# Two transformer layers on one core: transposes held back until the fourth row should be normalised, the next block's statistics started before, and a wait of Pool for the fourth normalisation

## The chip, the cores and the metric

One core of a Trainium2 chip runs the whole program. The metric is the device time of one execution in microseconds. The kernel before took 3607.83 us in the median of three runs (3604.56 to 3613.43). TensorE is called PE here, VectorE DVE, ScalarE ACT, GpSimd POOL, and SyncE, which issues nearly all DMAs, SP.

## The reference: two layers of attention and squared-ReLU MLP

The input is 2048 rows of 640 numbers in float32. Each of the two layers computes

```
n = layernorm(x);  q, k, v = n @ wqkv          (32 heads of 20)
x = x + concat_h(softmax(q k^T / sqrt(20)) v) @ wo
n = layernorm(x)
x = x + (relu(n @ w1 + b1) ** 2) @ w2 + b2     (1536 hidden)
```

The same weights serve both layers.

## The kernel before

Every float32 operand of a product is kept as a high and a low part, and a product is made of three: high by high, high by low, low by high. The part that the change touches is the first stage of a layer, in which rows are normalised, transposed and multiplied by wqkv.

**Blocks.** The 2048 rows are four blocks of 512, and a block is four tiles of 128 rows by 640. For a block, `front` (line 381) loads the four row tiles (SP, tile `x`, out of a pool of 11), computes the `stats` of each (line 239: two BATCH_NORM_STATS2 and one aggregate on DVE, then L247 and L248, variance plus eps to the power of -1/2, on POOL), and normalises each in place (L252, on DVE, tile `mv` holds mean and factor). Then 20 transposes on PE (L398) turn the block, five column groups k of four each, into PSUM banks: a group of two k, again two, then one. Each k is split from its bank into the high and low part of `xnT` by one of two ways: `split_to` (ACT casts, L256, and DVE subtracts, L257), or `split_on_pool` (ACT copies to `r`, L263, POOL casts, L271, and POOL subtracts, L274). For some k of blocks 2 and 3 it is POOL. Four banks in a ring (`ps_q`) serve the transposes and the scores.

**Products.** `qkv` (line 679) issues for each of the units (block, column tile of wqkv) a chain of 30 half matmuls (L327, 64 rows of the array each; two chains run in turns). `end_qk` (line 335) takes the finished sums of q or k out of the bank: ACT copies, POOL subtracts into the low part `ev` (L274) and, for k of the odd blocks, forms the difference of two blocks' keys in `kf` (L350) and splits it into `kd` (L271, L274). The tiles are stored to `d_qk` and `d_kd` by SP and loaded again as `k`, `q`, `kd` for the scores (L479). A score matmul fills a bank, and DVE takes the row maximum from it (L491).

**What sets the order.** The program is written out by a planner inside `qkv`. It keeps a model clock for PE, DVE and ACT (`now`); before each half matmul `insert` (line 804) may place one score operation or one group of transposes if the model says that the bank is free. The row work of the blocks is a generator, `rest`: `step_rest` takes one piece of it after every fourth step of the chains (loads, one `stats`, one normalisation), unless `state["turn"]` is set. It is set as soon as the fourth normalisation has been issued, and then the next free place takes the first group of transposes. `fronts` (line 410) loads the next block's rows at the eighth piece of a block. So in the program a block's evictions always stand ahead of the next block's statistics. In layer 1 (`begin_first`, line 1374) block 0 is done apart, and there alone the first POOL subtraction of the weights waits for the fourth normalisation (`lo_later`). In layer 2 (`second`, line 1357) only block 3 goes this way; blocks 0 to 2 arrive transposed from the stage before.

An engine works its own list in order; a wait holds all that is behind it on that engine.

Of the kernel before, what the change touches and what calls it, by code (L numbers as in the profile page):

```python
# [22 lines left out]
KD = D // P  # L23
# [16 lines left out]
def tile_layers(  # L40
# [11 lines left out]
    nc = tc.nc  # L52
# [45 lines left out]
    ps_q = Ring(0, 1, 2, 3)  # L98
# [16 lines left out]
    x_in = a_x[0]  # L115
    x_out = out[0]

    class Split:
# [132 lines left out]
    def normalise(eng, x, mv):  # L251
        return eng.tensor_scalar(x, x, mv[:, 0:1], mv[:, 1:2], op0=ALU.subtract, op1=ALU.mult)  # L252
# [17 lines left out]
    def pool_hi(dst, src):  # L270
        nc.gpsimd.tensor_copy(dst, src)  # L271

    def pool_lo(dst, a, b):
        nc.gpsimd.tensor_sub(dst, a, b)  # L274

    THREE = ((0, 0), (0, 1), (1, 0))

    def row_tile(src, r):
        t = xtile("x")
        dma(nc.sync, t, src[r * P : (r + 1) * P, :])  # L280
        return t
# [96 lines left out]
            v = vs.pop(tt)  # L378
            return lambda: dma(nc.sync, d_v[tt * P : (tt + 1) * P], v)

    def front(tb, x_src, bank, each=1, on_pool=()):

        rows = [row_tile(x_src, tb * 4 + i) for i in range(4)]
        yield 0, False
        mvs = []
        for x in rows:
            mvs.append(stats(x))
            yield 1.1, False
        for n, (x, mv) in enumerate(zip(rows, mvs)):
            normalise(nc.vector, x, mv)  # L390
            yield 0.65, n == 3
        res = []
        for k0 in range(0, KD, each):
            ks = range(k0, min(k0 + each, KD))
            dsts = [bank("xt") for _ in ks]
            for k, dst in zip(ks, dsts):
                for i in range(4):
                    nc.tensor.transpose(  # L398
                        dst[:, i * P : (i + 1) * P], rows[i][:, k * P : (k + 1) * P], ident
                    )  # L400
# [7 lines left out]
            yield 0, len(res) < KD  # L408

    def fronts(steps):  # L410


        for n, f in enumerate(steps):
            for m, cost in enumerate(f):
                if m == 7 and n + 1 < len(steps):
                    next(steps[n + 1])
                yield cost

    k_t, q_t, v_t, mx_t, kept = {}, {}, {}, {}, {}
    left, done, split = {}, set(), {}
# [252 lines left out]
    FIRST = 4  # L675
    UNITS = [(tb, pos) for tb in range(NQB) for pos in range(FIRST)]
    UNITS += [(tb, pos) for pos in range(FIRST, 10) for tb in range(NQB)]

    def qkv(first, x_src, rest, scores):

# [1 line left out]
        double, twos, begun = [], [], []  # L682
        left.update((t, 4) for t in range(NBLK))
        done.clear()
        state = {"n": 0, "turn": False, "op": None, "last": "one", "scores": True}
        now = {"pe": 0.0, "dve": 0.0, "act": 0.0}
        busy = [0.0] * 8
        early, late, soon = {}, {}, []
# [115 lines left out]
        def insert(par):  # L804


            op = state["op"]
            if bool(op) != bool(par):
                return False
            if now["pe"] < max(busy[b] for b in ps_q.coming(1)):  # L810
                return False
            if state["turn"] and not par:
                if now["pe"] < max(busy[b] for b in ps_q.coming(2)):
                    return False
                now["pe"] += 1.2
                for spot in ps_q.coming(2):
                    takes("act", 0.6, spot)
                    takes("dve", 0.7, spot)
                step_rest()
                return False  # L820
            if not op:
                if min(at_now) >= (len(chains) - 1) * N + 2 * N // 3:
                    if state["scores"]:
                        state["scores"] = False
                        next(scores)
                    return False
                op = state["op"] = choose()
                if not op:
                    return False
                state["last"] = op["kind"]  # L830
            single(op, par)
            if par:
                state["op"] = None
            return True

        def step_rest():
            cost, state["turn"] = next(rest, None) or (0, False)
            if cost:
                now["dve"] = max(now["dve"], now["pe"]) + cost

        chains = [{"of": ("qk", tb, pos)} for tb, pos in UNITS]
        for ch in chains[:2]:
# [54 lines left out]
        for j in range(len(chains)):  # L897
            if j < len(UNITS):
                while UNITS[min(j + 1, len(UNITS) - 1)][0] not in xt_:
                    step_rest()  # L900
                run(early, j)
            while min(at_now) < (j + 1) * N if j + 1 == len(chains) else at_now[0] < (j + 1) * N:
                for r in range(2) if j else (1, 0):
                    if not insert(r):
                        work_on(r)
                now["pe"] += 0.235 if j < len(UNITS) else 0.155
                state["n"] += 1
                if state["n"] % 4 == 0 and not state["turn"]:
# [448 lines left out]
    def second():  # L1357


        yield from front(3, d_x[1], ps_q, 2, (1, 3))  # L1360

    def constants():

# [10 lines left out]
    def begin_first():  # L1374

        rows = []
        for i in range(4):
            t = xtile("x")
            dma((nc.sync, nc.scalar)[i % 2], t, x_in[i * P : (i + 1) * P, :])
            rows.append(t)  # L1380
        for pos in range(FIRST):
            raws.append(raw_cols(wqkv, ORDER[pos]))
        yield
        dsts = [banks[:, k, :] for k in range(KD)]

# [17 lines left out]
        last = [normalise(nc.vector, rows[3], mvs[3])]  # L1403

        def lo_later(dst, a, b):
            m = nc.gpsimd.tensor_sub(dst, a, b)
            if last:
                after(m, last.pop(), "VectorE and Pool share a port")

        for pos in range(2):  # L1410
            w_qk.put(raws.pop(0), pos * 10, pos * 10 + KD, KD, nc.scalar.copy, lo_later)
        turn(3)
        again(6)
        rows.clear()
        steps = [front(tb, x_in, ps_q, 2, (1, 3)[: tb - 1]) for tb in (1, 2, 3)]
        next(steps[0])
        res = []
        for k in range(KD):
            t = slot([P, 2, QB], F32R, "xnT")
            split_to(t[:, 0, :], t[:, 1, :], dsts[k])  # L1420
            res.append(t)
            if k == KD - 1:
                xt_[0] = res
            yield 0, False
        yield from fronts(steps)

    b2_t = cpool.tile([P, D], F32, name="b2_t")
    opening = begin_first()
# [32 lines left out]
```

## Time and profile before

| | |
|---|---|
| runs | 3604.56, 3607.83, 3613.43 us |
| profiled execution | 3610.41 us |
| its span | 3608.6 us, mean granted clock 0.999 |
| PE busy | 3583.8 us (99%) |
| DVE, ACT, POOL busy | 76%, 73%, 22% |
| stage of the change | layer 1 from 15 to 100 us, layer 2 from 1820 to 1840 us |

A line of the timeline has the start in the span, the duration, the engine, the line of the kernel, the operation, out<-in, shapes, the count of equal instructions in a row, and in brackets the idle time of the engine before them with the instruction that ended it. The sum of the durations can exceed the distance of two starts, since matmuls overlap. PEclk or the granted clock is the share of TensorE's full clock that it was given.

### The profile page before, as it was taken

What the parts mean: (1) busy time and instruction counts of PE and PEld (TensorE: products, weight loads), DVE (VectorE), ACT (ScalarE), POOL (GpSimd) and SP (SyncE); (2) the same over time, 40 slices, a digit from 0 to 9 for tenths busy, and PEclk for the clock granted to TensorE, in tenths of its full rate; (3) what the DMA queues carried; (4) which work ended last, traced back from release to release, by engine and by line L of the source; (5) the groups of instructions that cost most, each with busy time, mean ns of one, the idle gap of its engine ahead of it and who ended that gap; (6) DMA issues with size and microseconds to landing.
All of it is one profiled execution on the core that took longest, in us unless ns stands there. A gap on an engine that the chain in (4) does not pass through costs nothing.

```text
span 3608.6 us, 67689 instructions
## 1 busy us (share of the span) xinstructions
PE 3583.8 (99%) x25562; PEld 2131.5 (59%) x25562; DVE 2752.8 (76%) x5081; ACT 2650.0 (73%) x5152; POOL 803.7 (22%) x880
## 2 busy tenths in 40 slices
PE   9999999999999999999999999999999999999999
PEld 7886434343434345999988963333443434368998
DVE  7877999999999993445567789999999999924443
ACT  3678999999999996122327789999999999942221
POOL 5531434311212211111144201211211211211110
PEclk9999999999999999999999999999999999999999
DMA  8866555323211125834577652222322111367221
GB/s 277 279 225 175 172 139 167 113 67 78 58 47 51 42 90 198 271 86 111 145 253 251 204 153 66 76 72 56 77 72 62 48 41 51 105 214 247 74 77 40
DMA packets 378117, 453.89 MB, mean 126 GB/s; under 512 B 176722, under 2 KB 224082, under 8 KB 377790
## 3 DMA queue, kind: packets, MB, share of 16 engines
q1 hardware_dynamic: 376974, 447.21, 41.4%
q8 instruction: 201, 3.29, 0.4%
q10 hardware_dynamic: 816, 2.36, 0.2%
q14 instruction: 126, 1.03, 0.1%
HBM read 275.14 MB, written 174.30 MB: 125 GB/s over the span
## 4 chain that ended last, share of the span: by engine, by line
PE 93%; DMA 3%; DVE 1%; POOL 1%; SPq 1%; ACT 1%; issue 0%; DVEq 0%; POOLq 0%; ACTq 0%
PE banks L573 27%; PE banks L561 19%; PE banks L479 16%; PE banks L289 12%; PE banks L327 9%; PE banks L1239 9%; SPq L76 1%; DMA q<-d_qk 1%; ACT e L568 0%; DVE bst L244 0%; PE banks L398 0%; DMA d_x<-x 0%; DMA few<-d_s 0%; DMA d_t<-y 0%; DMA o<-d_r 0%
## 5 line engine op out<-in xcount | busy, mean ns | idle before, releaser
L568 ACT ACTIVATE e<-banks 128x512 f32<-128x512 f32 x3968 | 2049.2, 604 | 67.7 <-PE banks L479 6.0
L491 DVE TENSOR_REDUCE mx<-banks 128x1 f32<-128x512 f32 x3076 | 1929.8, 683 | 211.7 <-PE banks L479 141.9
L479 PE MATMUL banks<-k,q 60*128 60x512 f32 x3586 | 1243.7, 428 | 2.9 <-DVE mx L491 1.4
L561 PE MATMUL banks<-q,k 62*128 62x512 f32 x3968 | 1116.6, 433 | 1.0 <-DVE mx L508 0.9
L573 PE MATMUL banks<-e,vg 128*32 128x512 f32 x8192 | 1091.0, 605 | 1.5 <-ACT e L1086 1.5
L561 PEld LDWEIGHTS banks<-q,k 62*128 62x128 f32 x3968 | 583.6, 185 | 656.0 <-ACT e L568 623.9
L479 PEld LDWEIGHTS banks<-k,q 60*128 60x128 f32 x3586 | 581.5, 184 | 292.0 <-DVE mx L491 217.6
L508 DVE CUSTOM_DVE_ANT_0 rl<-banks,rl 128x512 f32<-128x512 f32 x510 | 332.9, 688 | 102.2 <-PE banks L479 93.2
L327 PE MATMUL banks<-xnT,wqk 64*128 64x512 f32 x2400 | 381.1, 395 | 0.6 <-ACT mark_t L329 0.6
L573 PEld LDWEIGHTS banks<-e,vg 128*32 128x32 f32 x8192 | 161.1, 108 | 357.3 <-issue 331.0
L1224 ACT ACTIVATE r<-banks,b_t 128x512 f32<-128x512 f32 x96 | 66.2, 689 | 401.4 <-PE banks L289 378.9
L500 ACT ACTIVATE rl<-banks 128x512 f32<-128x512 f32 x512 | 271.9, 597 | 100.1 <-PE banks L479 93.6
L1239 PE MATMUL banks<-w,h 128*128 128x320 f32 x2304 | 340.4, 309 | 0.0
L1239 PEld LDWEIGHTS banks<-w,h 128*128 128x128 f32 x2304 | 339.1, 188 | 1.2
L289 PE MATMUL banks<-xnT,w 128*128 128x512 f32 x1440 | 329.4, 389 | 0.0
L327 PEld LDWEIGHTS banks<-xnT,wqk 64*128 64x128 f32 x2400 | 286.8, 186 | 35.5 <-issue 2.7
L289 PEld LDWEIGHTS banks<-xnT,w 128*128 128x128 f32 x1440 | 269.7, 188 | 55.2
L271 POOL CAST mr<-nt 128x32 fp32r<-128x32 f32 x64 | 13.4, 209 | 1121.4 <-DVE nt L534 1121.4
L617 POOL TENSOR_TENSOR few<-few,minus_t 128x16 f32<-128x16 f32 x62 | 179.8, 2900 | 232.0 <-DMA few<-d_s 231.9
L327 PE MATMUL banks<-wv,xnT 64*128 64x320 f32 x1920 | 199.9, 307 | 0.9 <-ACT mark_t L329 0.9
L327 PEld LDWEIGHTS banks<-wv,xnT 64*128 64x128 f32 x1920 | 188.2, 185 | 2.7 <-ACT mark_t L329 1.6
L1225 DVE TENSOR_TENSOR r<-r 128x512 f32<-128x512 f32 x96 | 75.6, 787 | 127.1 <-ACT r L1224 122.1
(83 smaller groups left out, 2020.1 us busy)
## 6 DMA issues: line engine op xcount, KB each, us to landing
q<-d_qk SPq DMA_DIRECT2D x242, 240.0 KB
d_qk<-ev SPq DMA_DIRECT2D x80, 512.0 KB
k<-d_qk SPq DMA_DIRECT2D x152, 240.0 KB
x<-d_x SPq DMA_DIRECT2D x88, 320.0 KB
d_qk<-ev SPq DMA_DIRECT2D x80, 256.0 KB
d_o<-ot SPq DMA_DIRECT2D x248, 80.0 KB
ot<-d_o SPq DMA_DIRECT2D x38, 512.0 KB
d_v<-v SPq DMA_DIRECT2D x32, 512.0 KB
```

Of the source, the lines that this page charges most:

```text
L289: nc.tensor.matmul(dst, a, b, start=(n == 0), stop=(n == last))
L327: m = nc.tensor.matmul(ch["dst"][:, :width], *pair, start=first, stop=last)
L479: nc.tensor.matmul(dst, q_t[t][b : b + 60, p, sub * P : (sub + 1) * P], k_t[t // NQB, c][b : b + 60, p, :], start=True, stop=True,)
L491: nc.vector.tensor_reduce(maxima(t)[:, 2 * par + p, sub, c : c + 1], dst, axis=AX.X, op=ALU.max)
L500: nc.scalar.activation(res, dst, AF.Relu)
L508: nc.vector.tensor_tensor_reduce(out=r, in0=dst, in1=r, scale=1.0, scalar=LEAST, op0=ALU.add, op1=ALU.max, accum_out=maxima(t)[:, 2 * par ...
L561: nc.tensor.matmul(dst, k_t[t // NQB, kt // 4][b : b + 62, p, (kt % 4) * P : (kt % 4 + 1) * P], q_t[t][b : b + 62, p, :], start=True, stop ...
L568: nc.scalar.activation(es[p][:, par, :], dst, AF.Exp, scale=SCALE)
L573: nc.tensor.matmul(acc[32 * h : 32 * h + 32, :], v_t[t // NQB, kt // 8][:, kt % 8, 32 * h : 32 * h + 32], es[p][:, par, :], start=(kt == 0 ...
L617: nc.gpsimd.tensor_tensor(few, few, minus_t, op=ALU.pow)
L1225: nc.vector.tensor_mul(r, r, r)
L1239: nc.tensor.matmul(dst[:, :HALF], hs[f][:, hx, i * P : (i + 1) * P], w_2.piece(at_2(f0 + f, hw, hf)), start=(f == 0 and (hx, hw) == THREE[0]),
```

## The change

It has three parts. A queue `turning` holds the transposes of a block until the planner's model clock of PE has passed the model time of the fourth normalisation on DVE by `READY` (0.9 us). Meanwhile `step_rest` goes on with the row work of the next block. And `pool_lo`, POOL's subtraction, waits for the fourth normalisation of a block if it is the first one that is written out after it (`last_row`); before, only block 0 had that. The loads of blocks 2 and 3 are placed anew: block 2's at the seventh piece of block 1, block 3's after block 1's last transposes.

```
     def pool_lo(dst, a, b):
-        nc.gpsimd.tensor_sub(dst, a, b)
+        m = nc.gpsimd.tensor_sub(dst, a, b)
+        if last_row:
[...]
...
-    def front(tb, x_src, bank, each=1, on_pool=()):
-        rows = [row_tile(x_src, tb * 4 + i) for i in range(4)]
-        yield 0, False
+    def rows_of_block(tb, x_src):
+        return [row_tile(x_src, tb * 4 + i) for i in range(4)]
+
+    def prepare(rows, turns):
         mvs = []
         for x in rows:
             mvs.append(stats(x))
-            yield 1.1, False
+            yield 1.1, None
         for n, (x, mv) in enumerate(zip(rows, mvs)):
-            normalise(nc.vector, x, mv)
-            yield 0.65, n == 3
+            m = normalise(nc.vector, x, mv)
+            if n == 3:
+                last_row.append(m)
+            yield 0.65, turns if n == 3 else None
+
+    def turns(tb, rows, bank, on_pool=(), then=None):
         res = []
...
+                if then:
+                    then()
+            else:
+                yield True
...
-            if state["turn"] and not par:
+            if turning and not par and now["pe"] >= turning[0][0]:
...
-                step_rest()
+                step_turn()
...
         def step_rest():
-            cost, state["turn"] = next(rest, None) or (0, False)
+            cost, turn = next(rest, None) or (0, None)
             if cost:
                 now["dve"] = max(now["dve"], now["pe"]) + cost
+            if turn:
+                turning.append((now["dve"] + READY, turn))
+
+        def step_turn():
+            if next(turning[0][1], None) is None:
+                turning.pop(0)
...
-                    step_rest()
+                    (step_turn if turning else step_rest)()
...
-                if state["n"] % 4 == 0 and not state["turn"]:
+                if state["n"] % 4 == 0:
                     step_rest()
...
+        def load(tb):
+            blocks[tb] = rows_of_block(tb, x_in)
+
+        for tb in (1, 2, 3):
+            x = blocks.pop(tb)
+            t = turns(tb, x, ps_q, (1, 3)[: tb - 1], (lambda: load(3)) if tb == 1 else None)
+            for n, cost in enumerate(prepare(x, t)):
+                if tb == 1 and n == 6:
+                    load(2)
+                yield cost
+            while tb == 2 and 3 not in blocks:
+                yield 0, None
```

In the order of the instructions, the number of each kind on DVE, POOL and SP is the same; PE has two score matmuls (L479) and ACT two activations (L500) fewer, at the end of layer 1's stage, of scores whose results nothing used. On PE, block 1's transposes come 14 half matmuls later than before, block 2's 26 later, and those of layer 2's block 3 14 later. Block 3's in layer 1 come later too, and something has moved ahead of them. Before, this is where they begin on PE (x_538 to x_544 are block 3's four row tiles; in brackets the engines that the instruction waits for):

```order
L327 MATMUL banks<-xnT_417,wqk_272 128x512
L327 MATMUL banks<-xnT_417,wqk_226 128x512
L398 MATMUL banks<-ident,x_538 128x128 [waits DVE_49]
L398 MATMUL banks<-ident,x_540 128x128 [waits DVE_49]
L398 MATMUL banks<-ident,x_542 128x128 [waits DVE_49]
L398 MATMUL banks<-ident,x_544 128x128 [waits DVE_49]
L398 MATMUL banks<-ident,x_538 128x128
L398 MATMUL banks<-ident,x_540 128x128
L398 MATMUL banks<-ident,x_542 128x128
L398 MATMUL banks<-ident,x_544 128x128
```

Now the row tiles of block 3 are x_459 to x_465, and the first four score matmuls stand 10 half matmuls ahead of them:

```order
L481 MATMUL banks<-k_591,q_594 128x512 [waits DMAHW7_49,DMAHW1_49,Activation_49]
L481 MATMUL banks<-k_591,q_594 128x512 [waits DMAHW2_49,DMAHW0_49,DVE_49]
L481 MATMUL banks<-k_591,q_594 128x512 [waits DVE_49] x2
...
L331 MATMUL banks<-xnT_422,wqk_230 128x512
L331 MATMUL banks<-xnT_619,wqk_223 128x512 [waits Pool_49]
L408 MATMUL banks<-ident,x_459 128x128 [waits DVE_49]
L408 MATMUL banks<-ident,x_461 128x128
L408 MATMUL banks<-ident,x_463 128x128
L408 MATMUL banks<-ident,x_465 128x128
L408 MATMUL banks<-ident,x_459 128x128 [waits DVE_49]
```

Before, the first four transposes wait each for its own row. Now the first of every group of four has a wait for DVE: for the reduction that empties its bank of a score.

On DVE these reductions stand behind block 3's normalisations, which follow block 2's evictions (`xnT_616` to `xnT_664`) and one statistics each way. The order before, from block 2's last eviction to block 3's normalisations:

```order
L257 TENSOR_TENSOR xnT_590<-banks,xnT_590 128x512 [waits Activation_49]
L244 BN_STATS bst_599<-x_538 128x6 [waits DMAHW0_49]
L244 BN_STATS bst_599<-x_538 128x6
L245 BN_AGGR mv_600<-bst_599 128x2 [waits DVE_49]
L244 BN_STATS bst_629<-x_540 128x6 [waits DMAHW1_49]
```

and now:

```order
L257 TENSOR_TENSOR xnT_637<-banks,xnT_637 128x512 [waits Activation_49]
L244 BN_STATS bst_644<-x_465 128x6 [waits DMAHW5_49]
L244 BN_STATS bst_644<-x_465 128x6
L245 BN_AGGR mv_645<-bst_644 128x2 [waits DVE_49]
L252 TENSOR_SCALAR x_459<-x_459,mv_555 128x640 [waits Pool_49]
L257 TENSOR_TENSOR xnT_664<-banks,xnT_664 128x512 [waits Activation_49]
L252 TENSOR_SCALAR x_461<-x_461,mv_570 128x640 [waits Pool_49]
L252 TENSOR_SCALAR x_463<-x_463,mv_600 128x640 [waits Pool_49]
L252 TENSOR_SCALAR x_465<-x_465,mv_645 128x640 [waits DVE_49,Pool_49]
L475 MEMSET mx_741 128x64
L493 TENSOR_REDUCE mx_741<-banks 128x1 [waits DVE_49,PE_49]
```

Three of block 3's four statistics have moved ahead of block 2's evictions, its first normalisation ahead of the last of them, and the first reductions ahead of block 3's own evictions. Block 2's statistics have moved in the same way: the first ahead of block 1's five evictions, the second behind the second of them.

POOL's list from the subtraction of `ev_679` on shows the only added wait of layer 1 (in layer 2 it stands on the subtraction of a part of block 3's `xnT`, which follows the transposes anyway). Now:

```order
L276 TENSOR_TENSOR ev_679<-r_680,ev_679 128x512 [waits Activation_49]
L354 TENSOR_TENSOR kf_378<-r_680,kf_378 128x512
L271 CAST kd_684<-kf_378 128x512 [waits Pool_49]
L276 TENSOR_TENSOR kd_684<-kf_378,kd_684 128x512 [waits Pool_49]
L276 TENSOR_TENSOR ev_725<-r_726,ev_725 128x512 [waits DVE_49,Activation_49]
L271 CAST xnT_771<-r_772 128x512 [waits Activation_49]
L276 TENSOR_TENSOR xnT_771<-r_772,xnT_771 128x512 [waits Pool_49]
```

Before, the subtraction of `ev_725` stood behind block 3's casts and waited for ACT alone. Around block 2's fourth statistics (`mv_496`) the first four rows read the same before but for the numbers. Now:

```order
L276 TENSOR_TENSOR ev_481<-r_482,ev_481 128x512 [waits Activation_49]
L247 TENSOR_TENSOR mv_496<-mv_496,eps_t 128x1 [waits DVE_49]
L248 TENSOR_TENSOR mv_496<-mv_496,half_t 128x1 [waits Pool_49]
L276 TENSOR_TENSOR ev_527<-kf_378,ev_527 128x512 [waits Activation_49]
L247 TENSOR_TENSOR mv_555<-mv_555,eps_t 128x1 [waits DVE_49]
```

`ev_481` and `ev_527` wait for ACT only. On SP, block 3's four row loads moved from behind the stores of the second q or k tile to ahead of the stores of the first, and the last of these loads waits for PE.

More of the change, by code (lines that the diff above doesn't have):

```diff
@@ L271, in pool_hi @@
         nc.gpsimd.tensor_copy(dst, src)
+    last_row = []
     def pool_lo(dst, a, b):
-        nc.gpsimd.tensor_sub(dst, a, b)
+        m = nc.gpsimd.tensor_sub(dst, a, b)
+        if last_row:
+            after(m, last_row.pop(), "VectorE and Pool share a port")
     THREE = ((0, 0), (0, 1), (1, 0))
@@ L387, in front @@
             mvs.append(stats(x))
-            yield 1.1, False
+            yield 1.1, None
         for n, (x, mv) in enumerate(zip(rows, mvs)):
-            normalise(nc.vector, x, mv)
-            yield 0.65, n == 3
+            m = normalise(nc.vector, x, mv)
[3 more added lines that the diff above has]
+    def turns(tb, rows, bank, on_pool=(), then=None):
         res = []
-        for k0 in range(0, KD, each):
-            ks = range(k0, min(k0 + each, KD))
+        for k0 in range(0, KD, 2):
+            ks = range(k0, min(k0 + 2, KD))
             dsts = [bank("xt") for _ in ks]
@@ L407, in front @@
                 rows.clear()
[L408 to L417, printed above, removed]
+                if then:
+                    then()
+            else:
+                yield True
     k_t, q_t, v_t, mx_t, kept = {}, {}, {}, {}, {}
@@ L677, in tile_layers @@
     UNITS += [(tb, pos) for pos in range(FIRST, 10) for tb in range(NQB)]
+    READY = 0.9
     def qkv(first, x_src, rest, scores):
@@ L684, in qkv @@
         done.clear()
-        state = {"n": 0, "turn": False, "op": None, "last": "one", "scores": True}
+        state = {"n": 0, "op": None, "last": "one", "scores": True}
+        turning = []
         now = {"pe": 0.0, "dve": 0.0, "act": 0.0}
@@ L1357, in second @@
     def second():
-        yield from front(3, d_x[1], ps_q, 2, (1, 3))
+        x = rows_of_block(3, d_x[1])
+        yield 0, None
+        yield from prepare(x, turns(3, x, ps_q, (1, 3)))
     def constants():
@@ L1402, in begin_first @@
             again(6)
[L1403 to L1408, printed above, removed]
+        last_row.append(normalise(nc.vector, rows[3], mvs[3]))
         for pos in range(2):
-            w_qk.put(raws.pop(0), pos * 10, pos * 10 + KD, KD, nc.scalar.copy, lo_later)
+            w_qk.put(raws.pop(0), pos * 10, pos * 10 + KD, KD, nc.scalar.copy, pool_lo)
         turn(3)
@@ L1414, in begin_first @@
         rows.clear()
-        steps = [front(tb, x_in, ps_q, 2, (1, 3)[: tb - 1]) for tb in (1, 2, 3)]
-        next(steps[0])
+        blocks = {1: rows_of_block(1, x_in)}
         res = []
@@ L1423, in begin_first @@
                 xt_[0] = res
-            yield 0, False
-        yield from fronts(steps)
+            yield 0, None
+        def load(tb):
[8 more added lines that the diff above has]
+            while tb == 2 and 3 not in blocks:
+                yield 0, None
     b2_t = cpool.tile([P, D], F32, name="b2_t")
```

## The prediction

> **What bounds the kernel now.** I read the page first, then the waits of TensorE between 10 and 130 us, then the timeline of each engine around the lines the diff touches.
>
> ```profile
> span 3608.6 us, 67689 instructions
> PE 3583.8 (99%) x25562; PEld 2131.5 (59%) x25562; DVE 2752.8 (76%) x5081; ACT 2650.0 (73%) x5152; POOL 803.7 (22%) x880
> PE 93%; DMA 3%; DVE 1%; POOL 1%; SPq 1%; ACT 1%; issue 0%; DVEq 0%; POOLq 0%; ACTq 0%
> ```
>
> TensorE is busy 99% of the span and makes up 93% of the chain that ended last. The waits list adds the place (columns: total, times, longest):
>
> ```profile
> PE banks L398 <- DVE x L252: 4.0, 6, 1.3
> ```
>
> So the change can only win what TensorE stands still, or runs at less than full clock, around the transposes (L398) of four blocks: three in layer 1, one in layer 2. These are the passes of blocks 1 and 2; the columns are start, duration, and in brackets the idle time before with its releaser.
>
> ```profile
> 21.16 0.61 PE L398 MATMUL banks<-ident,x 128*128 128x128 f32 x2
> 23.63 0.77 PE L398 MATMUL banks<-ident,x 128*128 128x128 f32 x5 [1.34 <-DVE x L252]
> 28.57 6.89 PE L327 MATMUL banks<-xnT,wqk 64*128 64x512 f32 x58
> 35.56 0.33 PE L398 MATMUL banks<-ident,x 128*128 128x128 f32 x1
> 38.08 1.33 PE L398 MATMUL banks<-ident,x 128*128 128x128 f32 x5 [1.14 <-DVE x L252]
> 43.47 7.33 PE L327 MATMUL banks<-xnT,wqk 64*128 64x512 f32 x62
> ```
>
> Block 1's pass (20 transposes and 6 half matmuls between them) takes 28.57 - 21.16 = 7.41 us, block 2's (10 half matmuls between) 43.47 - 35.56 = 7.91 us. What would a pass take that waits for nothing? Block 3's pass, at full clock, tells it:
>
> ```profile
> 50.73 0.55 PE L398 MATMUL banks<-ident,x 128*128 128x128 f32 x3
> 52.23 0.76 PE L398 MATMUL banks<-ident,x 128*128 128x128 f32 x5 [0.95 <-DVE x L252]
> 52.92 0.51 PE L327 MATMUL banks<-xnT,wqk 64*128 64x512 f32 x2
> 53.36 1.09 PE L398 MATMUL banks<-ident,x 128*128 128x128 f32 x8
> 54.38 0.73 PE L327 MATMUL banks<-xnT,wqk 64*128 64x512 f32 x4
> 55.05 0.66 PE L398 MATMUL banks<-ident,x 128*128 128x128 f32 x4
> 55.63 2.11 PE L327 MATMUL banks<-xnT,wqk 64*128 64x512 f32 x16
> ```
>
> From start to start, eight transposes take 54.38 - 53.36 = 1.02 us (0.128 each), two matmuls 0.44, four 0.67, the last four transposes 0.58. A pass without a wait is 1.02 + 0.44 + 1.02 + 0.67 + 0.58 = 3.73 us. Block 3's took 55.63 - 50.73 = 4.90, so it waited 1.17. Block 1's took 3.68 too long. For block 2, four more matmuls at 7.33 / 62 = 0.118 us make the bare pass 4.20, and 3.71 is excess.
>
> The excess is of two kinds. The fourth transpose of block 1 would have begun at 21.16 + 3 x 0.128 = 21.54 and began at 23.63: 2.09 us of waiting. The other 1.59 is the clock, as the windows show (columns: length; busy time of PE, PEld, DVE, ACT, POOL with counts; granted clock; DMA share; GB/s):
>
> ```profile
> 20.99:24.41 3.42, 1.89 (x14) 1.03 (x10) 2.52 (x3) 1.38 (x4) 2.22 (x2) 1.00 0.80 317
> 24.41:27.83 3.42, 3.42 (x14) 2.22 (x14) 2.18 (x4) 1.83 (x4) 0.00 (x0) 0.50 0.87 341
> 34.65:38.07 3.42, 1.80 (x11) 0.76 (x7) 3.30 (x4) 1.08 (x3) 2.94 (x4) 1.00 0.60 213
> 38.07:41.48 3.41, 3.40 (x14) 2.64 (x15) 0.69 (x1) 1.44 (x3) 1.31 (x2) 0.50 0.97 295
> 1829.92:1833.33 3.41, 2.27 (x18) 1.65 (x17) 1.82 (x2) 1.48 (x3) 1.42 (x3) 1.00 0.52 204
> 32.00:36.00 4.00, 3.79 (x33) 2.66 (x29) 3.93 (x10) 1.53 (x4) 3.50 (x7) 1.00 0.02 4
> 36.00:52.00 16.00, 13.86 (x94) 10.64 (x94) 11.50 (x23) 5.23 (x11) 9.22 (x15) 0.89 0.98 322
> ```
>
> Stretches in which PE was busy only 1.89 and 1.80 us are each followed by one at clock 0.50; layer 2's, with 2.27 busy, is not. Block 2's excess likewise splits into 38.08 - (35.56 + 0.38) = 2.14 of waiting and 1.57 of clock.
>
> What they wait for is the normalisation of the fourth row, and what holds that is DVE and POOL together:
>
> ```profile
> 20.30 3.27 DVE L252 TENSOR_SCALAR x<-x,mv 128x640 f32<-128x640 f32 x4
> 33.92 4.10 DVE L252 TENSOR_SCALAR x<-x,mv 128x640 f32<-128x640 f32 x4
> 33.88 1.28 POOL L274 TENSOR_TENSOR ev<-r,ev 128x512 fp32r<-128x512 f32 x1
> 36.41 1.26 POOL L274 TENSOR_TENSOR ev<-kf,ev 128x512 fp32r<-128x512 f32 x1
> ```
>
> Four normalisations take 3.27 us in block 1 and 4.10 in block 2, where two POOL subtractions of 1.27 lie inside.
>
> **The change, part by part.** Blocks 1 and 2 of layer 1. By the order, block 1's transposes come 14 half matmuls later, 14 x 0.118 = 1.65 us. They start at 22.81, the fourth would follow at 23.19, and its row is there at 23.63 as before (DVE and POOL have the same work in the same order up to there): 0.44 us of waiting stays. With that little, PE is busy about 3.0 of the 3.42 us and keeps its clock. Term: **-3.68 + 0.44 = -3.24**. Block 2's come 26 later: PE arrives at 35.56 - 3.24 + 26 x 0.118 = 35.4, the fourth transpose at 35.8. The statistics of its four rows now start before block 1's evictions, not after them, and the last normalisation is estimated to end by 35: **-3.71**. If both POOL subtractions fall on the normalisations again and the statistics win nothing, the row comes at 38.0, 2.2 us late with a half clock behind it: that end is 0.
>
> The added wait on Pool. In blocks 1 and 2 and layer 2, the POOL subtraction that lies on the normalisations is issued ahead of the fourth, so it gets no wait (the order shows none). It costs nothing there and frees nothing. Only in block 3 does one subtraction wait for DVE; behind it on POOL stand block 3's own casts and subtractions, which come after the transposes anyway. Cost 0, at most one 1.27 us subtraction; taken as 0.
>
> Block 3 gets a new kind of wait. The first four score matmuls (L479) now stand ahead of its transposes and take the four banks, and each group of four transposes waits for a reduction on DVE that stands behind block 3's normalisations. PE's arrival at the scores: 50.73 + 10 x 0.118 - 6.95 = 45.0; ten matmuls and four scores later, at about 46.6, the first transposes. DVE: row 4's statistics need POOL's L247/L248, which stand behind a subtraction of block 2, and the last three normalisations then run against these:
>
> ```profile
> 50.56 1.27 POOL L274 TENSOR_TENSOR ev<-r,ev 128x512 fp32r<-128x512 f32 x1
> 51.78 1.52 POOL L350 TENSOR_TENSOR kf<-r,kf 128x512 f32<-128x512 f32 x1
> 58.01 9.66 DVE L491 TENSOR_REDUCE mx<-banks 128x1 f32<-128x512 f32 x16 [0.88 <-PE banks L479]
> 67.84 15.63 DVE L491 TENSOR_REDUCE mx<-banks 128x1 f32<-128x512 f32 x26
> ```
>
> Moved by 6.95 they begin at about 43.6. Three normalisations beside 1.27 + 1.5 + 0.6 + 1.3 us of POOL end, I estimate, at 47.1, and the first reduction (9.66 / 16 = 0.60 us) at 48.4. That is 1.8 us of waiting, and a little at the next groups: 2.05, against 1.17 before: **+0.88**. Ends: -1.17 (DVE is early) and +2.5 (POOL always first: 3.7 of waiting); a half clock behind it would add 1.6.
>
> Then what is late next. Between 58 and 83.5 DVE runs 42 reductions back to back, so it is DVE's start that carries the gain on. It starts at 47.9 in place of 58.0, but pays the first four reductions and three evictions before scores flow again at about 54; the fifth reduction comes at 54.3, in place of 58.01 + 4 x 0.60 = 60.4. That is 6.1 earlier, the same as the PE side's 6.95 - 0.88. At the end of that stretch PE waits for a DMA:
>
> ```profile
> 83.92 0.47 PE L479 MATMUL banks<-kd,q 60*128 60x512 f32 x1 [1.55 <-DMA q<-d_qk]
> 36.12 2.54 SPq L76 DMA_DIRECT2D x<-in_A_x_dram  x4
> ```
>
> The q comes behind stores released by POOL's kd work, which moves along by the same 6; I keep the 1.55. If it went: -1.55.
>
> SP's queue. Block 3's four loads (36.12) now stand ahead of the stores of the first two k/q tiles; the last waits for PE's last transposes of block 1 (about 26.2), and the stores wait behind it. From 32 to 36 the DMA share was 0.02, so there is room: 13 transfers of 5.2 MB at 322 GB/s take 16.3 us, and the first score operands land at 42.5, ahead of 45.0. Cost 0.
>
> Two score matmuls and two activations fewer at the end of layer 1's stage: at 0.47 each between 0 and -0.94, since a neighbour can run beside them; **-0.5**.
>
> Layer 2's block 3:
>
> ```profile
> 1823.19 5.05 PE L327 MATMUL banks<-xnT,wqk 64*128 64x512 f32 x42 [0.28 <-ACT mark_t L329]
> 1831.10 0.77 PE L398 MATMUL banks<-ident,x 128*128 128x128 f32 x5 [1.14 <-DVE x L252]
> 1834.51 5.74 PE L327 MATMUL banks<-xnT,wqk 64*128 64x512 f32 x48
> 1829.43 1.26 POOL L274 TENSOR_TENSOR ev<-kf,ev 128x512 fp32r<-128x512 f32 x1
> ```
>
> From 1828.24 to 1834.51 are 6.27 us, 2.54 over the bare pass, with no drop of the clock. 14 matmuls are done first: **-1.65**. The remaining 0.89 stays, since POOL's subtraction at 1829.43 still blocks the fourth row.
>
> Sum: -3.24 - 3.71 + 0.88 - 0.5 - 1.65 = **-8.2 us**. The profiled execution took 3610.41 us (3608.6 of span, 1.8 around it), 2.6 above the median of the three runs, 3607.83. So 3602.2 in its terms, and 3599.6 in the median's.
>
> [...] The half clock goes only if waiting caused it, and the rows above (1.80 and 1.89 us busy against 2.27) say it did. [...]
>
> **The rivals.** (A) The forecast. (B) Block 3 waits for nothing, and the q wait of 1.55 goes too: -8.2 - 2.05 - 1.55 = -11.8, 3596.0. For it: POOL's kd work may come before or after the normalisations. Against: the order puts the reductions in between. (C) The clock still drops in both passes: -8.2 + 1.59 + 1.57 = -5.0, 3602.8. [...] (D) Slower: the loads of block 3 block SP. If the last one's tile comes free not at 26.2 but with block 2's last transposes (about 40), the 5.2 MB begin there, q lands at 56.4, and the first score waits 11.4 us, with two half-clock stretches (3.2): 14.6 on top, and PE, not DVE, is late at block 3 (-0.9): -8.2 + 13.7 = +5.5, 3613.3. It turns the sign from a landing at about 53 on. Against it: 11 row tiles, and the order's row waits for PE only. (E) Layer 1's gain is lost where DVE and the DMA set the pace (58 to 100 us): what stays is 0.5 + 1.65 = 2.2, 3605.6. For it: PE waits for a DMA at 83.92. Against: the DMAs that pace it are released by the work that moves. (F) The change does not do what it says: the Pool wait is empty in three of four places, which A already has; if block 2's fourth row moves back along with the transposes (its end of 0, +3.7) and block 3 takes its worst (2.5 + 1.6 - 0.88 = +3.2), what stays is -8.2 + 6.9 = -1.3, 3606.5. For it: two POOL subtractions still stand among block 2's normalisations; against: its statistics start earlier.
>
> **How the numbers follow.** Chances: A 0.52, B 0.14, C 0.09, D 0.06, E 0.10, F 0.09. A's own range comes from block 3's ends (-2.05 and +1.6) and the two score matmuls (0.5): -10.8 to -6.1. The range for 8 in 10 takes in B below and E above, and a spread as that of the three runs (4 us): 3593 to 3609. A measurement of this kernel can tell 0.3% from no change, 10.8 us. Faster by more than that: B and the low edge of A, 0.20. Slower by more: only D with the stall longer than worked out, 0.04. Within: 0.76.
>
> **What the profile after would show.** Right: one wait of about 0.4 us for L252 near 23, none near 36, no stretch at clock 0.50 between 20 and 45, transposes of block 3 waiting about 2 us for L491's reductions near 47, the q wait near 78, layer 2's pass 1.65 shorter. Wrong: a stretch at 0.50 although no wait is left (C); a first score waiting for a DMA near 45 (D); the row of 83.92 not earlier than 81 (E); block 2's fourth transpose still waiting 1 us or more (F).

## The result and the profile after

The changed kernel takes 3594.16 us in the median of six runs (3591.45 to 3596.07), beside 3608.52 us of the kernel before (3604.56 to 3613.43, six runs). The ratio is 0.9958, with a 95% interval of 0.9947 to 0.9969: 15 us faster, between 11 and 19. The time lies inside the forecast range, 5.4 us below the value forecast: the direction was right, and the gain nearly twice the 8.2 us that were worked out. To a gain of more than 10.8 us the forecast had given a chance of 0.20. A second series gave 3594.40 us (0.9960, 0.9947 to 0.9974).

The time goes with the mean granted clock of an execution. Of 54 executions of the kernel before that ran beside the experiments (one more, at a clock of 0.278, took 11961 us and is left out), those at 1.000 took 3604.5 us in the median, those at 0.999 3607.1, at 0.998 3610.7 and at 0.997 3611.7. The ten executions of the changed kernel at 1.000, out of its two series, took 3594.1 us in the median. By this estimate some 10 us of the gain are left at an equal clock, and the other 4 or so came with the clock.

The profiled execution took 3596.07 us, with a span of 3594.3: 14.3 us less than that of before. TensorE in the timeline of the changed kernel, through the three passes of layer 1:

```profile
17.75 4.95 PE L331 MATMUL banks<-xnT,wqk 64*128 64x512 f32 x42
22.63 0.55 PE L408 MATMUL banks<-ident,x 128*128 128x128 f32 x3
23.53 0.77 PE L408 MATMUL banks<-ident,x 128*128 128x128 f32 x5 [0.35 <-DVE x L252]
...
26.94 8.23 PE L331 MATMUL banks<-xnT,wqk 64*128 64x512 f32 x70
35.10 1.09 PE L408 MATMUL banks<-ident,x 128*128 128x128 f32 x8
...
39.74 5.06 PE L331 MATMUL banks<-xnT,wqk 64*128 64x512 f32 x42
44.64 1.00 PE L481 MATMUL banks<-k,q 60*128 60x512 f32 x4
45.27 1.52 PE L331 MATMUL banks<-xnT,wqk 64*128 64x512 f32 x10
46.98 1.26 PE L408 MATMUL banks<-ident,x 128*128 128x128 f32 x8 [0.18 <-DVE mx L493]
...
50.86 2.12 PE L331 MATMUL banks<-xnT,wqk 64*128 64x512 f32 x16
```

Block 1 waits 0.35 us for its fourth row, where it waited 1.34 before, block 2 not at all, and block 3 has 0.18 us in a wait of a new kind, for a reduction. The same stretches as before, in the same columns, all have clock 1.00:

```profile
20.99:24.41 3.42, 3.07 (x26) 2.11 (x22) 3.31 (x6) 1.36 (x5) 2.11 (x2) 1.00 1.00 401
24.41:27.83 3.42, 3.42 (x26) 2.34 (x27) 3.38 (x8) 2.22 (x5) 1.49 (x4) 1.00 0.16 44
38.07:41.48 3.41, 3.41 (x30) 2.43 (x30) 3.38 (x7) 0.83 (x2) 3.25 (x5) 1.00 0.95 275
```

Layer 2's pass, and the first wait for q, with what was left of it:

```profile
1819.56 0.55 PE L408 MATMUL banks<-ident,x 128*128 128x128 f32 x3
1820.82 0.77 PE L408 MATMUL banks<-ident,x 128*128 128x128 f32 x5 [0.71 <-DVE x L252]
...
1824.21 13.69 PE L331 MATMUL banks<-xnT,wqk 64*128 64x512 f32 x118
```

```profile
76.04 0.47 PE L481 MATMUL banks<-kd,q 60*128 60x512 f32 x1 [0.88 <-DMA q<-d_qk]
```

Where the 14.3 us arose is seen by taking the start of the same instruction in both traces, before minus after (median over a stretch, times of the kernel before):

| place | gain by then | of it here | forecast |
|---|---|---|---|
| start (17 us) | 0.1 | 0.1 | |
| block 1's pass (30) | 3.25 | 3.1 | 3.24 |
| block 2's pass (47) | 7.3 | 4.0 | 3.71 |
| block 3 and DVE's stretch (74) | 7.45 | 0.2 | -0.88 |
| wait for q and those behind it (98) | 8.3 | 0.85 | 0 |
| end of layer 1's stage (313 to 322) | 9.8 | 1.4 | 0.5 |
| layer 1's turn from attention to MLP (1475) | 10.2 | 0.3 | 0 |
| layer 2's pass (1840) | 11.9 | 1.7 | 1.65 |
| layer 2's waits for q (1890) | 11.5 | -0.3 | 0 |
| end of layer 2's stage (2113) | 12.5 | 0.8 | 0 |
| layer 2's turn to MLP (3268) | 14.35 | 2.0 | 0 |

(Block 2's row is 43.47 + 30 x 0.118 - 39.74 = 7.3, since 30 more half matmuls lie before the end of the pass in the changed kernel. The 0.2 us missing in the sum lie between the rows.)

### The profile page after: what moved, and what is told of

Read it like the earlier page. It is cut to its first block, busy times and chain, and to the rows that moved or that the text cites. A ratio compares the mean times of both kernels' runs of the same rounds, so it can differ in the third digit from the quotient of the medians.

```text
span 3594.3 us, 67684 instructions
## 1 busy us (share of the span) xinstructions
PE 3576.5 (100%) x25560; PEld 2127.4 (59%) x25560; DVE 2755.3 (77%) x5081; ACT 2649.0 (74%) x5150; POOL 805.5 (22%) x880
## 4 chain that ended last, share of the span: by engine, by line
PE 95%; DVE 1%; DMA 1%; ACT 1%; issue 1%; POOL 1%; SPq 0%; ACTq 0%; DVEq 0%; POOLq 0%
PE banks L575 28%; PE banks L563 19%; PE banks L481 16%; PE banks L293 13%; PE banks L1249 9%; PE banks L331 9%; DMA q<-d_qk 1%; PE banks L1089 1%; ACT e L570 0%; DVE bst L244 0%; SPq L76 0%; DVE x L252 0%; ACT e L1096 0%; DVE xnT L257 0%; DMA d_qk<-ev 0%
```

## The experiments

Theory W, the forecast's: the gain comes from half matmuls that now stand where TensorE waited for its rows, the clock included, and the added wait of POOL does nothing. Rival P: it comes from POOL kept off the normalisations. A third: from the earlier loads and statistics. And five rows of the table were put at 0 by the forecast.

**Without the added wait.**

```
-            m = normalise(nc.vector, x, mv)
-            if n == 3:
-                last_row.append(m)
+            normalise(nc.vector, x, mv)
```

> The changed kernel without the added waits of POOL (block 0 keeps its own); the order of every engine is that of the changed kernel. Theory W (the gain comes from half matmuls that now stand where TensorE waited, and the added wait is empty): the whole gain of 14 us stays, within 1.5 us, and the normalisations of blocks 1 to 3 and of layer 2 take as long as in the changed kernel (3.3, 4.1, about 5 and, in layer 2, the fourth 1.4 us). Theory P (the gain comes from POOL kept off the normalisations): the gain shrinks by 3 us or more, with longer waits of the transposes.

3594.89 us, ratio to before 0.9965 (0.9953 to 0.9978): the gain of the changed kernel, within the interval. By 74 us the gain is 7.49, against 7.45 with the wait. In the one profile of this run TensorE then does not wait for the first q at all (0.88 and 0.90 us in the two profiles of the changed kernel). POOL's rows up to there differ by 0.1 us at most, and two profiles of another program, the one with both edits below, waited 1.38 and 0.79 there, so this is taken for chance; it was not tested further.

**The added wait alone.** The kernel before, with the changed kernel's `pool_lo` and `last_row`.

> The kernel before with the added waits of POOL alone, as the change writes them; nothing is reordered. W: no difference, 0 within 2 us, the fourth transpose of blocks 1 and 2 still waits 2.1 us and the half-clock stretches stay. P: 3 us or more are gained.

3606.51 us, ratio 1.0000 (0.9990 to 1.0009). Up to 78 us no instruction moves by more than 0.1 us in the median, and the half-clock stretches stay (the first, from 24.55 to 27.96, has a granted clock of 0.50). The list of waits (total, times, longest, 10 to 130 us) has the line that the kernel before has:

```profile
PE banks L404 <- DVE x L252: 4.0, 6, 1.3
```

As written, the wait is empty. Rival P falls as an account of this change.

**The wait made effective, transposes at their old places.** What is left of a block's statistics and normalisations is issued ahead of a q or k eviction that falls among them; the planner's steps then skip what was issued ahead, so that the transposes stay where they were.

```
...
             if what == "qk":
+                while preparing:
+                    cost, turn = next(rest)
+                    now["dve"] = max(now["dve"], now["pe"]) + cost
+                    state["ahead"] = state.get("ahead", 0) + 1
                 pending.append(end_qk(b, a, dst))
...
```

> The kernel before, transposes at their old places, but what is left of a block's statistics and normalisations is issued ahead of a k or q eviction that falls among them, so that POOL's subtraction does wait for the fourth normalisation. [...] The fourth transpose then comes 1.0 us earlier in block 1, 1.6 in block 2, about 1.2 in block 3 and 1.0 in layer 2: 4.8 us of waiting gone. If the half clock is set by PE's waiting, both half-clock stretches go as well, another 3.2: -8 us in all. If the clock follows the transposes and not the waits, -4.8 and the stretches at 0.50 stay. If DVE and POOL do not hinder each other, 0.

3600.72 us, ratio 0.9981 (0.9972 to 0.9991): 7 us faster, between 3 and 10. So there is a second way to shorten the same waits. DVE's and POOL's rows, blocks 1 and 2:

```profile
20.18 2.29 DVE L252 TENSOR_SCALAR x<-x,mv 128x640 f32<-128x640 f32 x4
31.29 2.29 DVE L252 TENSOR_SCALAR x<-x,mv 128x640 f32<-128x640 f32 x4
```

```profile
22.61 1.27 POOL L276 TENSOR_TENSOR ev<-kf,ev 128x512 fp32r<-128x512 f32 x1 [0.79 <-DVE x L252]
33.72 1.27 POOL L276 TENSOR_TENSOR ev<-r,ev 128x512 fp32r<-128x512 f32 x1 [0.79 <-DVE x L252]
```

Four normalisations take 2.29 us alone, 3.27 with one POOL subtraction among them, 4.10 with two: each costs DVE 0.9 to 1.0 us of its own 1.27. What holds DVE up then was not shown. The waits of layer 1's passes shrink from 4.0 to 0.9 us in all, no stretch up to 74 us has half clock (1.00 from 20 to 30 and from 36 to 68 us), and by 74 us the gain is 6.85, nearly the changed kernel's 7.45. But then part of it is given back, at the row of rival E:

```profile
77.85 0.47 PE L488 MATMUL banks<-kd,q 60*128 60x512 f32 x1 [2.33 <-DMA q<-d_qk]
```

The q comes late for a TensorE that is early, and a stretch after it loses the clock as well (0.50 from 78.19 to 81.61): from 98 us on the gain is 4.57. The changed kernel, whose loads for block 3 stand ahead of the stores, waited 0.88 there; whether that is due to the loads was not tested apart.

**Not held back.** The changed kernel with one number changed.

```
-    READY = 0.9
+    READY = -10
```

> The changed kernel with READY at -10: transposes are issued as soon as their normalisations are, blocks 1 and 2 and layer 2's block 3 at the places they had before; rows still go on meanwhile and the loads stand as in the changed kernel. W: waits of about 2 us and half-clock stretches come back in blocks 1 and 2, layer 2's 2.5 us too, the time is that of the kernel before within 3 us. If the earlier loads and statistics were what counts, at least half of the 14 us stays.

3603.54 us, ratio 0.9989 (0.9980 to 0.9999): some 4 us of the 15 stay, where 3 at most were expected. By 74 us the gain is -0.5. So none of the first 7.5 us comes from the earlier loads and statistics by themselves; it takes the later place of the transposes. Whether that place would win it all without the earlier statistics was not run. What stays arises later: 2.0 between 100 and 210 us, whose cause was not found, 1.4 at 313 to 322 us as in the changed kernel, and 3.4 at layer 1's turn to the MLP (below). Layer 2's pass takes 1.7 back: it has a half-clock stretch there (0.50 from 1825.48 to 1828.89), which the profile of before had not.

This run also tells where the half-clock stretches fall. Its stretches (columns as in the forecast):

```profile
19.83:23.24 3.41, 2.00 (x13) 0.98 (x9) 3.30 (x6) 1.15 (x3) 2.84 (x4) 1.00 1.02 405
23.24:26.66 3.42, 3.33 (x14) 2.57 (x15) 1.42 (x3) 1.37 (x3) 0.00 (x0) 0.50 0.37 142
33.48:36.90 3.42, 2.61 (x19) 1.52 (x15) 3.35 (x5) 1.14 (x3) 3.34 (x5) 1.00 0.79 305
36.90:40.31 3.41, 2.57 (x19) 1.96 (x21) 1.61 (x3) 1.83 (x4) 1.42 (x3) 1.00 1.03 404
40.31:43.72 3.41, 3.41 (x30) 2.50 (x28) 3.38 (x8) 1.30 (x4) 1.66 (x3) 1.00 0.96 269
47.14:50.55 3.41, 1.76 (x14) 1.05 (x11) 2.15 (x2) 0.73 (x3) 3.33 (x5) 1.00 0.61 231
50.55:53.96 3.41, 3.41 (x16) 2.31 (x14) 0.97 (x2) 1.80 (x4) 3.19 (x5) 0.50 0.60 235
```

Block 2 waits 1.14 us for its fourth row here as in the kernel before, where a half-clock stretch followed. Here the wait, which ends at 37.74, lies across 36.90, the edge of two of these stretches of 3.41 us; each is busy 2.6 us, and no half clock follows; it comes in block 3's pass instead. Within a trace the half-clock stretches begin a whole number of 3.41 us apart: in the kernel before at 24.41 and, 4 x 3.41 later, at 38.07, in this run at 23.24 and, 8 x 3.41 later, at 50.55. That such a grid of 3.41 us runs on between them, so that 36.90 is one of its edges, and that it starts elsewhere in each execution, is an estimate from these starts.

**The two score operations.** The kernel before without the last score operation that layer 1's stage begins and never finishes.

```
-                if len(begun) < 2:
+                if len(begun) < 2 and not (first and state.get("steps") == 127):
                     w = following(double, twos)
                     if w:
+                        state["steps"] = state.get("steps", 0) + 1
```

> The kernel before without the last score operation that layer 1's stage begins and never finishes (two score matmuls, two activations, as the change drops them); all else before 300 us stands as it was. Prediction's term: -0.5 us at the end of layer 1's stage. Rival, from the two traces: the gain that appeared there between 313 and 322 us (1.4 us) comes from these two whole operations, because ACT and the bank are free for attention earlier: -1.4, and perhaps 0.8 more at the end of layer 2's stage. Third: the 1.4 came from elsewhere: 0.

In time it is 3606.17 us, ratio 0.9993 (0.9984 to 1.0003), which tells nothing by itself. The traces do: this execution ran 1.54 us behind the profiled one of before from 90 to 313 us (it ran at half clock from 37.73 to 44.56, two stretches where before had one), and 0.09 behind from 322 us on: 1.45 us gained at this place alone. Another 0.74 us came at the end of layer 2's stage (0.90 to 1.64), as in the changed kernel. ScalarE before and here, where the exponentials of attention (`e`) begin:

```profile
317.02 2.07 ACT L500 ACTIVATE rl<-banks 128x512 f32<-128x512 f32 x4 [1.06 <-PE banks L479]
320.37 2.06 ACT L568 ACTIVATE e<-banks 128x512 f32<-128x512 f32 x4 [1.28 <-issue]
```

```profile
318.57 1.09 ACT L500 ACTIVATE rl<-banks 128x512 f32<-128x512 f32 x2 [1.06 <-PE banks L479]
320.29 2.24 ACT L568 ACTIVATE e<-banks 128x512 f32<-128x512 f32 x4 [0.63 <-issue]
```

Two activations of 0.5 us fewer stand ahead of them, and TensorE's first attention scores stand a few matmuls earlier in the program too. Which of the two is the larger was not separated, nor why layer 2's end, whose order is unchanged, gains as well.

**No scores ahead of block 3's transposes.**

```
                 step_turn()
+                return False
+            if not op and turning:
                 return False
             if not op:
```

> The changed kernel, but no score operation is begun while transposes are queued, so that block 3's transposes come first again. Prediction's view (the scores ahead of them cost a wait for DVE's reductions): as fast as the changed kernel or up to 2 us faster. Rival (DVE sets the pace from there to the first wait for q, so four reductions done early are a gain): the reductions end about 2.4 us later, the q wait shrinks, and the kernel is 1 to 2.4 us slower than the changed one.

3600.65 us, ratio 0.9980 (0.9971 to 0.9990): 6 us slower than the changed kernel, more than either view said. Up to 74 us it is ahead (gain 8.3 against 7.45, although this execution started 0.6 us later), so the scores ahead do cost 1.4 us there, as the forecast had it in kind; with a q wait of 1.8 us its gain is the changed kernel's by 98 us. Of the 6 us, 5.5 are lost between 322 and 1430 us (gain 8.1 to 2.6): the planner fits two paired score operations fewer into the stage, and attention has single scores to do in their place, as the groups between 322 and 1430 us show (busy, mean, idle before), first of the changed kernel, then of this one:

```profile
L493 DVE TENSOR_REDUCE mx<-banks 128x1 f32<-128x512 f32 x1464 | 919.1, 684 | 91.8 <-PE banks L481 55.6 <-PE banks L563 34.9
```

```profile
L493 DVE TENSOR_REDUCE mx<-banks 128x1 f32<-128x512 f32 x1475 | 925.3, 683 | 93.4 <-PE banks L481 57.6 <-PE banks L563 34.5
```

Eight reductions more in the whole program, at 0.68 us, would make 5.5 us; that this is the loss is argued, not shown. For it speaks that the two profiles of the next kernel, with one paired operation fewer than the changed kernel and four reductions more, lose 1.6 to 1.8 us there, and the two of the changed kernel 0.3 at most. It is a side effect of this edit, and the run doesn't price the order of block 3 beyond 98 us.

**Held back, and the wait made effective.** The edit of the run with the wait made effective, in the changed kernel.

> [...] What the changed kernel still waits for its rows is 0.35 us in block 1 and 0.7 in layer 2: at most 1 us faster than the changed kernel. If the gain of keeping POOL off and that of holding the transposes back added up, 6 us faster.

3591.65 us, ratio 0.9956 (0.9941 to 0.9971). Waits for normalised rows (L252) are gone from the list, in both layers. How its time compares with the changed kernel's is told in the last experiment.

**Held back longer.** READY at 1.9.

> The changed kernel with READY at 1.9 in place of 0.9: transposes 6 to 10 half matmuls later again (0.7 to 1.2 us). The rest of 0.35 us of waiting in block 1 and 0.7 in layer 2 goes: at most 1 us faster than the changed kernel; block 3's transposes come later too, two more scores stand ahead of them, and if its evictions then hold up the chains, up to 1 us slower.

3591.55 us, ratio 0.9960 (0.9945 to 0.9975): in time no different from the changed kernel, with four runs. The profiled execution is ahead of it by 1.1 us at 74 us and by 2.1 at 340 us, more than expected, and by another 0.9 in layer 2's pass; it then shows layer 1's turn to the MLP at its worst, 3.9 us of waiting.

**The two best beside each other.**

> The changed kernel once more, as a measure beside the next run and as a second profile of it. The layers' turns from attention to the MLP (near 1470 and 3255 us) should again show a wait for L1164 of another length than before, with or without a stretch at half clock, although nothing is changed there; the gains up to 340 us and between 1800 and 2150 us should be the same within 0.5 us (theory: those are the change's, the two turns are chance).

> The changed kernel with POOL's wait made effective, once more, on the chip of the run before. If the 2.5 us by which its median lay under the changed kernel's are real: 2 to 3 us faster than that. If the score mix that its planner chose takes the gain back between 330 and 1430 us: within 1 us.

The changed kernel: 3594.40 us (3591.70 to 3596.09). With the effective wait: 3591.43 us (3589.81 to 3591.76), ratio to before 0.9952 (0.9939 to 0.9964). All but one of the changed kernel's five runs lie above all five of the other: 3 us faster, more than the 1 us first expected and less than the 6 of two gains that add up, and the lowest ratio here. The edit was worth 1.9 us by 74 us (9.3 against 7.4) and 0.7 to 0.9 more in layer 2; part is given back in attention (gain 12.3 at 330 us, 10.6 at 1450).

The second profile of the changed kernel repeats the gains of the table: 3.22, 7.42, 8.24, 9.80 up to 340 us, then 1.5 in layer 2's pass and 0.85 at the end of its stage. One row does not repeat: layer 2's waits for q win 0.8 here and lost 0.3 there, so that the gain from 1800 to 2150 us differs by 1.0, twice what was expected. What differs most are the turns from attention to MLP, where TensorE waits for the attention's output that goes through DMAs (L1164). These rows are layer 1's turn in the two profiles of the changed kernel:

```profile
1470.56 6.20 PE L293 MATMUL banks<-wo,ot 128*128 128x320 f32 x30 [2.55 <-DVE x L1164]
```

```profile
1469.67 4.66 PE L293 MATMUL banks<-wo,ot 128*128 128x320 f32 x30 [1.24 <-DVE x L1164]
```

Thirty matmuls take 6.20 us after the long wait, where the granted clock is 0.72 in the mean from 1470.56 to 1476.76, and 4.66 after the short one. Over all profiles this wait was 0 to 3.9 us, and 0 to 1.9 in layer 2; within the changed kernel it was 2.55 and 1.24 in layer 1, 0 and 1.1 in layer 2.

## Why the forecast was right, and where it was off

**Blocks 1 and 2, layer 2's pass.** Right in mechanism and size: 3.1, 4.0 and 1.7 against 3.24, 3.71 and 1.65. The run that isn't held back loses the first two whole by 74 us: block 1's at once, block 2's partly (gain 1.9 at 47 us), since its wait fell across the edge of two stretches, each busy 2.6 us, with no half clock behind, and the rest with the half clock that came later. The remaining waits were forecast at 0.44 and 0.89 and measured at 0.35 and 0.71.

**The clock.** Right that the half clock goes with the waiting, and rival C falls: the changed passes, which wait 0 to 0.71 us for their rows, have a clock of 1.00. But the 3.16 us of it in the sum were no fixed price. They are what the half clock cost in that one execution. The run without the two score operations, whose order is that of before in these passes, had three half-clock stretches in layer 1 and one in layer 2's pass. The forecast took layer 2's to be free of them; that the profile of before showed none there is taken for chance, by the estimate of the grid above. The executions sorted by their clock, above, put the clock's part of the whole gain at about 4 us.

**The added wait on POOL.** Right: empty (the run without it and the run with it alone). The step that took POOL's work as the holder of the fourth row was right as well: keep it away and the waits of layer 1's passes shrink from 4.0 to 0.9 us.

**Block 3.** Wrong in sign: +0.88 forecast, -0.2 measured. The step that failed is the start of the last three normalisations, taken as 43.6 us by moving POOL's rows of before along with TensorE:

```profile
42.46 3.60 DVE L252 TENSOR_SCALAR x<-x,mv 128x640 f32<-128x640 f32 x3
46.02 0.11 DVE L475 MEMSET mx<- 128x64 f32 x1
46.23 2.48 DVE L493 TENSOR_REDUCE mx<-banks 128x1 f32<-128x512 f32 x4
```

They began at 42.46 and took 3.6 us, near the 3.5 expected, so the first reduction came at 46.2 in place of 47.8, just when TensorE arrived. POOL was not tied to TensorE in these microseconds: its eviction at 42.64 followed row 4's L248 at once.

```profile
42.07 0.55 POOL L248 TENSOR_TENSOR mv<-mv,half_t 128x1 f32<-128x1 f32 x1
42.64 1.57 POOL L276 TENSOR_TENSOR ev<-r,ev 128x512 fp32r<-128x512 f32 x1
```

**The wait for q** was 0.88 us, where the forecast kept 1.55; three profiles in the order of before have 1.55 to 1.92. Part of that is chance (1.38 and 0.79 in two profiles of one program). Rival E's mechanism is real, as the run with the wait made effective shows, but here the row came at 76.04 and little was lost; why the changed kernel escapes it stays open.

**The other rivals.** B is the nearest in time (3596.0): block 3 hardly waits, as it said, but of the q wait less than half went. D did not occur: the first scores, at 44.64, waited for no DMA. F did not either: block 2's fourth transpose waits for nothing.

**The two score operations**: mechanism seen, size off by three: 0.5 forecast, 1.45 measured at the place and 0.74 later.

**The turns to the MLP**: 2.3 us of the difference of the two profiles. The second profile of the changed kernel has 3.2 and 0, so most of this is chance; whether some is the change's stays open, for in layer 2 the three profiles in the order of before waited 1.3 to 1.9 us and the three in the changed order 0 to 1.1. The forecast was right on the passes, then, and its time fell inside the range with the help of gains that it had put at nothing. That the two profiles differ by as much as the medians do is partly luck: the profile of before lies 1.9 us above the median of its six runs, that of after 1.9 above its own, so the chance parts cancel about evenly, and which parts of the medians they stand for stays open.

## What to carry to other kernels

A transposition that waits for rows in an otherwise full TensorE cost the wait here (2.09 and 2.14 us in the kernel before) and, in some executions, a half-clock stretch on top (1.59 and 1.57); moving it behind work that was ready anyway removed both here, and no price was seen up to 98 us. Look in the order whether an added wait lands on the instruction that collides: this one did only when the normalisations were issued ahead of it. Count what a planner drops or repacks at the end of a stage: two matmuls and two activations there were worth more than their own durations, and a plan with two paired scores fewer went with a loss of 5.5 us in the next stage.

## What the runs showed of the hardware

Half clock came behind stretches of 3.41 us in which TensorE was busy up to 2.07 us, and the busy time of a stretch does not draw the line. The first of these four rows, of the run with the added wait alone, is a stretch of matmuls only, busy 1.75 us, and the clock stays at 1.00 in the next. The third, of the run without the two score operations (layer 2's pass), nearly all transposes, is busy 2.07 us, and the next is at 0.50:

```profile
82.58:86.00 3.42, 1.75 (x16) 1.73 (x17) 0.92 (x3) 2.07 (x5) 1.26 (x1) 1.00 1.05 368
86.00:89.41 3.41, 3.41 (x30) 2.72 (x28) 3.22 (x9) 0.66 (x2) 0.00 (x0) 1.00 1.01 376
1826.32:1829.73 3.41, 2.07 (x13) 1.31 (x13) 2.30 (x3) 1.07 (x2) 1.50 (x3) 1.00 0.35 141
1829.73:1833.14 3.41, 3.41 (x16) 2.10 (x14) 0.78 (x2) 1.22 (x3) 3.25 (x4) 0.50 0.25 95
```

Part of the difference may lie in the view, for a transpose that stands alone is shown with 0.33 us (at 35.56 in the kernel before), while in a row they follow each other every 0.128 us. No run varied the busy time on purpose, and where the line lies was not shown.

In the kernel before, TensorE issues nothing but transposes up to 12.31 us, and 24 of them follow each other every (6.61 - 1.36) / 24 = 0.22 us at first, six a little later every (8.20 - 7.55) / 6 = 0.11. Later in the same trace eight transposes took 26.91 - 25.01 = 1.90 us at clock 0.50 and 1.02 at 1.00, 0.24 and 0.128 each. By these spacings the clock rose on transposes alone; that is an estimate, since the view gives 1.00 from the start:

```profile
1.36 5.38 PE L1388 MATMUL banks<-ident 128*128 128x128 f32 x24 [1.36 <-POOL ident masks.py:199]
6.61 1.10 PE L1392 MATMUL banks<-ident,x 128*128 128x128 f32 x5
7.55 0.82 PE L1388 MATMUL banks<-ident 128*128 128x128 f32 x6
8.20 0.71 PE L1392 MATMUL banks<-ident,x 128*128 128x128 f32 x5
```
